# A fused attention and SwiGLU block: a new written-out instruction order for all five engines

## The chip, the cores and the metric

The kernel runs on one core of one Trainium2 chip. Its five engines work from queues of their own: TensorE (PE in the profile) multiplies matrices into PSUM, VectorE (DVE), ScalarE (ACT) and GpSimd (POOL) work on SBUF and PSUM, and SyncE (SP) issues DMA transfers. Each queue runs in order; semaphores hold an instruction until what it needs from another engine or a transfer is done. The metric is the device time of one execution in microseconds (us), lower is better.

## What is computed

```python
def reference(A_x, A_wqkv, A_wo, B_x, B_w1, B_w3, B_w2, c, w_mod):
    # x: 1 x 2048 x 512 in bf16; 32 heads of 16; window 8, dilation 2; F = 1792
    ...
    qkv = x @ wqkv                      # of the modulated layer norm of x
    idx = pos[:, None] - arange(8) * 2  # 8 keys behind each position, every second one
    logits = einsum('bhsd,bhswd->bhsw', q, k[idx]) * scale   # masked where idx < 0
    o = einsum('bhsw,bhswd->bhsd', softmax(logits), v[idx])
    attention = o @ wo
    ...
    out = (silu(h @ w1) * (h @ w3)) @ w2
```

The block around these two is an adaptive layer norm: a vector c gives, through w_mod, a shift, a scale and a gate for each half. So x becomes x + gate_a * attention(LN(x) * (1 + scale_a) + shift_a), and then x + gate_b * ffn(LN(x) * (1 + scale_b) + shift_b). The output is bf16 in the form of x.

## The kernel before, in words

The 2048 positions are 16 tiles of 128. Python code first records 1118 operations (class Program), each with its engine, and with the values that it reads and writes; nothing is issued yet. The recorded work goes through these stages.

First layer norm: statistics (L555, L556 on DVE), variance and power (L563, L565 on POOL), normalizing (L576 on DVE); then a transpose on PE (L636) or by DMA, and the modulation while draining (L644, L621 on ACT). Projections: q and k by L691 (drained by L700 and L701 on ACT), v by L711 (drained by L721), which goes to a scratch in HBM.

Attention, tile by tile and mostly two tiles to a softmax: the elementwise product of q with eight shifted k on DVE (L742, 128x4096), its sum over each head by tiled matmuls (L752; L749 for the first tile), maximum and subtraction on DVE (L764, L769), exp on ACT (L782), sum, reciprocal and scaling on DVE (L794, L796, L797), a transpose on PE (L807) with its copy on ACT (L811), the product with the gathered v on DVE (L827, 128x4096; the gathers are DMAs by L124 on SP), the sum over the window by tiled matmuls (L855), a copy on ACT (L861), a transposing DMA that SP issues (sb_ot), the output projection on PE (L867), and the residual with its row sum on DVE (L871).

Second layer norm, for two tiles at a time: POOL makes the negative mean (L586); ACT squares each of the two tiles with a row sum (L590); POOL makes the variance (L596), its power (L597) and the bias (L599); ACT normalizes each (L601). Then transposes (L636, or by DMA) and modulation (L644, L621). The FFN goes over six groups of tiles, two or four tiles each ([0,1], [2,3], [4..7], [8..11], [12,13], [14,15]): for each of 14 slices of F gate and up (L883, 128x256 or 128x512), silu on ACT (L889), the product on DVE (L892); then w2 (L921, L909 for the last two tiles), the addition on DVE (L931) and the store.

What sets the order of the work: a list, ORDER, written out at the end of the file, holds the numbers of the 1118 operations. `place` (L145) goes through it once and appends each operation to the queue of its engine, so ORDER sets each queue's sequence. A second list, SLOTS, says for each pooled value which buffer or PSUM bank it takes, and the values that share one follow each other in ORDER. `synchronize` then derives the waits: an operation waits for what it reads, and for the last users of a buffer that it takes over. Between engines nothing else is enforced; how two operations on different engines stand in ORDER has no meaning in itself.

```python
        for at, o in enumerate(self.placed):
            o.at = at
            o.pos = len(self.order[o.eng])
            self.order[o.eng].append(o)
            for v in o.vals:
                if v.pool is not None and v.pool.last.get(v.slot) is not v:
                    before = v.pool.last.get(v.slot)
                    if before is not None:
                        o.prev.extend(before.users)
                    v.pool.last[v.slot] = v
```

Of the kernel before, what the change touches and what calls it, by code (L numbers as in the profile page):

```python
# [272 lines left out]
def _build(p, A_x, A_wqkv, A_wo, B_w1, B_w3, B_w2, c, w_mod, out):  # L273
# [710 lines left out]
    143, 142, 144, 145, 90, 146, 147, 148, 107, 173, 171, 174, 108, 172, 109, 110, 111, 181, 179, 114, 115, 175, 176, 116, 125, 126,  # L984
    127, 128, 129, 130, 182, 121, 153, 180, 154, 156, 155, 112, 177, 150, 178, 149, 152, 151, 117, 135, 131, 132, 133, 134, 229,
    122, 123, 136, 137, 113, 183, 184, 185, 138, 186, 163, 164, 237, 161, 235, 165, 238, 139, 236, 187, 193, 140, 166, 227, 228,
    189, 239, 194, 195, 188, 41, 196, 197, 198, 190, 167, 331, 230, 332, 159, 287, 168, 240, 241, 242, 231, 232, 233, 246, 333, 289,
    157, 191, 192, 211, 118, 209, 288, 234, 244, 290, 199, 162, 339, 281, 158, 160, 347, 245, 212, 210, 243, 203, 205, 200, 215,
    216, 204, 349, 169, 348, 350, 279, 340, 218, 334, 280, 351, 206, 219, 282, 352, 353, 381, 341, 372, 291, 292, 293, 342, 207,
    294, 221, 354, 355, 250, 249, 362, 247, 369, 224, 213, 336, 248, 359, 361, 214, 201, 360, 257, 258, 283, 284, 285, 202, 371,  # L990
    356, 370, 357, 358, 253, 254, 208, 273, 276, 286, 259, 260, 170, 265, 266, 217, 261, 379, 298, 380, 363, 364, 222, 277, 365,
    220, 382, 373, 374, 43, 37, 375, 295, 255, 274, 263, 297, 296, 267, 223, 256, 264, 301, 411, 413, 270, 268, 335, 412, 49, 262,
    300, 366, 414, 299, 251, 252, 383, 415, 384, 275, 376, 302, 367, 368, 416, 385, 403, 271, 44, 417, 377, 378, 602, 603, 402, 404,
    604, 311, 312, 269, 303, 317, 318, 386, 387, 309, 310, 388, 304, 401, 418, 605, 307, 308, 606, 389, 390, 607, 609, 608, 337,
    278, 315, 392, 313, 314, 322, 325, 445, 225, 338, 615, 610, 614, 616, 394, 611, 393, 613, 612, 305, 391, 328, 306, 329, 443,
    316, 444, 405, 406, 319, 617, 622, 626, 407, 446, 627, 395, 396, 397, 419, 420, 623, 477, 45, 634, 635, 447, 642, 618, 272, 320,
    46, 636, 637, 628, 629, 619, 620, 621, 52, 226, 326, 51, 630, 631, 408, 624, 625, 344, 638, 448, 421, 422, 50, 640, 639, 641,
    662, 670, 644, 643, 645, 449, 409, 646, 410, 450, 632, 647, 47, 633, 654, 398, 399, 451, 663, 666, 400, 671, 672, 452, 48, 343,
    650, 655, 668, 667, 669, 648, 649, 682, 683, 684, 453, 652, 651, 653, 435, 656, 657, 664, 433, 436, 685, 454, 665, 673, 658,
    678, 434, 437, 321, 426, 686, 687, 689, 695, 688, 694, 691, 660, 323, 659, 661, 423, 478, 475, 696, 424, 438, 425, 697, 690,  # L1000
    692, 674, 693, 742, 439, 730, 465, 731, 466, 468, 743, 427, 744, 745, 726, 706, 708, 707, 709, 476, 479, 467, 469, 428, 458,
    429, 710, 711, 456, 457, 712, 713, 722, 723, 724, 727, 728, 729, 455, 732, 733, 440, 725, 430, 746, 698, 699, 459, 53, 702, 703,
    480, 54, 470, 471, 472, 734, 735, 441, 442, 460, 461, 345, 346, 714, 431, 432, 738, 762, 462, 481, 497, 482, 473, 474, 483, 675,
    676, 747, 763, 463, 464, 704, 498, 484, 764, 765, 499, 715, 487, 716, 717, 700, 701, 718, 720, 509, 770, 771, 679, 705, 750,
    736, 737, 490, 748, 772, 485, 719, 500, 749, 488, 721, 739, 740, 752, 741, 507, 766, 767, 769, 489, 779, 768, 751, 754, 753,
    486, 501, 773, 774, 778, 775, 776, 780, 777, 781, 782, 491, 785, 758, 759, 760, 327, 783, 755, 529, 502, 510, 508, 492, 784,
    798, 818, 511, 512, 503, 531, 532, 680, 830, 493, 513, 330, 530, 831, 521, 539, 832, 514, 515, 820, 822, 814, 799, 815, 522,
    819, 504, 505, 516, 517, 541, 494, 324, 520, 495, 518, 506, 834, 806, 786, 807, 496, 761, 836, 794, 833, 823, 835, 677, 821,
    838, 858, 808, 859, 681, 533, 534, 559, 519, 523, 535, 809, 837, 540, 558, 542, 543, 524, 860, 525, 570, 790, 796, 795, 788,
    797, 545, 861, 791, 810, 787, 789, 802, 792, 793, 526, 544, 536, 547, 546, 549, 548, 862, 537, 569, 538, 550, 803, 527, 528,  # L1010
    839, 863, 864, 804, 805, 811, 551, 594, 812, 813, 866, 824, 825, 867, 800, 567, 593, 552, 553, 554, 874, 592, 868, 869, 826,
    557, 816, 560, 801, 840, 827, 870, 871, 555, 872, 568, 556, 817, 876, 841, 865, 854, 875, 561, 873, 846, 877, 828, 571, 842,
    595, 881, 562, 572, 829, 577, 563, 584, 855, 879, 578, 579, 564, 573, 850, 856, 580, 574, 878, 880, 906, 908, 581, 596, 565,
    566, 575, 576, 954, 857, 585, 907, 583, 909, 918, 919, 894, 582, 586, 843, 956, 955, 957, 886, 887, 958, 756, 898, 587, 588,
    895, 597, 890, 891, 589, 926, 847, 598, 599, 959, 960, 962, 899, 900, 901, 927, 961, 848, 590, 600, 591, 601, 1032, 910, 920,
    921, 963, 964, 965, 892, 893, 967, 966, 1034, 928, 1033, 1035, 1036, 1037, 851, 968, 852, 849, 972, 974, 976, 978, 973, 980,
    929, 911, 984, 986, 977, 979, 975, 844, 845, 985, 987, 853, 1039, 988, 990, 989, 1038, 930, 931, 932, 981, 982, 983, 933, 902,
    904, 991, 903, 905, 970, 934, 969, 1040, 896, 897, 971, 882, 1041, 888, 889, 884, 883, 922, 885, 923, 935, 936, 924, 946, 1043,
    1042, 942, 937, 938, 950, 1004, 1006, 1005, 1007, 1000, 1045, 1002, 1001, 925, 1008, 1012, 1009, 1013, 1016, 1017, 996, 998,
    997, 914, 999, 915, 1018, 992, 1003, 1044, 993, 994, 1014, 1015, 1019, 995, 916, 757, 912, 917, 1024, 913, 939, 1028, 940, 1070,  # L1020
    1090, 1071, 1086, 1072, 1073, 1091, 1010, 1087, 1074, 1011, 1082, 1075, 1088, 941, 1083, 1078, 1089, 1079, 1092, 1093, 1094,
    1084, 1096, 1095, 1097, 1080, 1081, 943, 951, 1085, 952, 944, 947, 948, 949, 1054, 1050, 1066, 1051, 1052, 1053, 953, 945, 1020,
    1062, 1064, 1076, 1077, 1063, 1046, 1067, 1068, 1069, 1047, 1055, 1056, 1057, 1021, 1022, 1023, 1058, 1060, 1059, 1061, 1029,
    1048, 1025, 1098, 1049, 1030, 1065, 1099, 1100, 1101, 1110, 1111, 1112, 1114, 1115, 1113, 1116, 1117, 1026, 1027, 1102, 1031,
    1103, 1104, 1105, 1106, 1107, 1108, 1109,
]
SLOTS = [
    7, 0, 1, 2, 3, 4, 5, 6, 0, 1, 2, 3, 4, 5, 6, 7, 0, 1, 2, 3, 4, 5, 6, 7, 0, 3, 4, 5, 6, 0, 1, 1, 0, 2, 3, 0, 4, 0, 7, 1, 0, 2, 1,
    2, 3, 6, 1, 5, 0, 7, 5, 7, 6, 2, 2, 1, 4, 0, 1, 3, 1, 2, 0, 4, 1, 4, 0, 7, 5, 1, 3, 6, 3, 0, 4, 2, 0, 1, 2, 1, 1, 0, 2, 4, 0, 1,
    2, 1, 4, 3, 6, 5, 1, 1, 0, 1, 3, 2, 3, 2, 4, 0, 0, 2, 3, 4, 1, 0, 3, 5, 6, 5, 1, 5, 3, 3, 2, 2, 0, 2, 6, 1, 2, 0, 3, 6, 7, 5, 3,  # L1030
    0, 1, 1, 0, 6, 0, 1, 1, 0, 0, 0, 0, 0, 1, 1, 5, 1, 6, 0, 1, 1, 1, 0, 5, 1, 0, 3, 1, 5, 0, 2, 3, 1, 4, 0, 2, 4, 2, 100, 5, 1, 2,
    5, 1, 1, 0, 1, 4, 0, 7, 1, 0, 4, 0, 1, 1, 1, 1, 5, 0, 7, 0, 0, 1, 1, 6, 0, 1, 1, 1, 0, 5, 1, 0, 0, 100, 7, 0, 2, 1, 1, 6, 0, 2,
    6, 2, 100, 5, 1, 1, 3, 1, 3, 0, 2, 5, 0, 4, 1, 0, 0, 1, 0, 1, 6, 0, 0, 6, 1, 0, 4, 1, 7, 0, 2, 6, 6, 1, 0, 0, 1, 1, 6, 100, 2,
    0, 0, 2, 1, 4, 7, 2, 1, 5, 103, 2, 102, 3, 101, 6, 103, 1, 100, 4, 101, 5, 104, 2, 106, 4, 102, 3, 100, 3, 105, 2, 104, 1, 102,
    4, 105, 1, 100, 3, 108, 5, 104, 2, 109, 4, 105, 7, 110, 5, 102, 7, 113, 5, 103, 6, 111, 2, 102, 6, 107, 6, 101, 1, 112, 0, 100,
    3, 102, 0, 3, 2, 0, 4, 4, 104, 0, 101, 1, 105, 1, 102, 1, 105, 7, 115, 1, 103, 4, 116, 7, 100, 2, 100, 5, 101, 7, 105, 7, 101,
    5, 119, 2, 102, 1, 117, 7, 100, 7, 118, 5, 103, 2, 103, 4, 100, 5, 106, 5, 104, 4, 114, 2, 102, 0, 104, 6, 104, 4, 107, 2, 101,
# [38 lines left out]
```

## Time and profile before

| | us |
|---|---|
| median of 3 runs | 239.26 (239.23 to 241.12) |
| the profiled execution, its own time | 240.36 |
| span of the profiled execution, first to last instruction | 238.6 |
| the two transposing DMAs that the chain of waits goes through | 4.29 and 3.71 |

The granted TensorE clock is 1.00 throughout. In the profile's timeline a line gives the start in us, the duration, the engine, the line of the kernel, the operation, the tiles written and read, and how many alike stand in a row; in brackets stands how long the engine was idle before, and on whom it waited. The chain of waits is followed back from the last instruction: each line has a start, a share of time, and the engine and line that held the end at that moment.

### The profile page before, as it was taken

How to read it: one execution, taken by the hardware profiler on the slowest of the kernel's cores; microseconds unless marked ns; L12 is line 12 of the kernel's file. 1: busy time of each engine (PE TensorE's matmuls, PEld its weight loads, DVE VectorE, ACT ScalarE, POOL GpSimd, SP SyncE). 2: the span in 40 equal slices, each digit the busy share in tenths (PEclk: the TensorE clock that was granted, in tenths of full speed). 3: DMA queues.
4: the chain of work that ended last, by engine and by line, in shares of the span. 5: the costliest groups of instructions: out<-in, count | busy, mean ns of one | idle time of the engine just before them, and what ended most of it. 6: DMA issues, size and time to landing. Idle time of an engine off the chain costs nothing.

```text
span 238.6 us, 4560 instructions
## 1 busy us (share of the span) xinstructions
PE 232.2 (97%) x1806; PEld 136.7 (57%) x1806; DVE 179.4 (75%) x279; ACT 138.3 (58%) x267; POOL 28.8 (12%) x66
## 2 busy tenths in 40 slices
PE   7999999999999998999999999999899999999995
PEld 4776554545688683664444444444375457485874
DVE  5699999999999999899999999690653403434433
ACT  2289587899978737776765594747553406040300
POOL 4434000013002000240003420020010000000000
PEclk9999999999999999999999999999999999999999
DMA  6999999999999996876972783634303000000202
GB/s 216 372 330 309 157 242 301 217 288 315 302 293 254 247 203 178 240 180 193 229 220 62 192 209 76 166 113 46 67 5 104 3 0 0 3 22 0 69 1 88
DMA packets 46317, 38.85 MB, mean 163 GB/s; under 512 B 21704, under 2 KB 37080, under 8 KB 46296
## 3 DMA queue, kind: packets, MB, share of 16 engines
q1 hardware_dynamic: 46288, 38.56, 65.1%
q8 instruction: 14, 0.23, 0.4%
q14 instruction: 7, 0.06, 0.1%
q10 hardware_dynamic: 8, 0.00, 0.0%
HBM read 29.62 MB, written 4.21 MB: 142 GB/s over the span
## 4 chain that ended last, share of the span: by engine, by line
PE 83%; DMA 8%; DVE 3%; SPq 3%; ACT 1%; issue 0%
PE pall L883 40%; PE pall L921 17%; PE pall L691 7%; PE pall L867 5%; DMA sb_x<-in_A_x_dram 5%; PE pall L711 4%; DMA sb_ot<-sb_ac 3%; PE pall L752 3%; SPq L124 3%; PE pall L855 3%; PE pall L909 3%; DVE sb_pq L742 2%; DVE sb_st L555 1%; PE pall L807 1%; DVE sb_xn L576 1%; ACT sb_ac L861 0%
## 5 line engine op out<-in xcount | busy, mean ns | idle before, releaser
L883 PE MATMUL pall<-sb_h,sb_w 128*128 128x256 bf16 (+1 forms) x672 | 102.6, 308 | 0.0
L883 PEld LDWEIGHTS pall<-sb_h,sb_w 128*128 128x128 bf16 x672 | 65.0, 98 | 35.7 <-issue 2.5
L889 ACT ACTIVATE sb_sg<-pall 128x256 bf16<-128x256 f32 (+1 forms) x84 | 35.6, 454 | 54.5 <-PE pall L883 53.4
L892 DVE TENSOR_TENSOR sb_hh<-sb_sg,pall 128x256 bf16<-128x256 bf16 (+1 forms) x84 | 40.0, 505 | 36.1 <-PE pall L883 34.0
L921 PE MATMUL pall<-sb_w,sb_hh 128*128 128x512 bf16 x196 | 44.9, 379 | 0.0
L742 DVE TENSOR_TENSOR sb_pq<-sb_q,sb_kT 128x4096 bf16<-128x4096 bf16 x16 | 36.3, 2282 | 0.0
L921 PEld LDWEIGHTS pall<-sb_w,sb_hh 128*128 128x128 bf16 x196 | 19.0, 98 | 21.6 <-DVE sb_hh L892 0.4
L691 PE MATMUL pall<-sb_h,sb_wqkv 128*128 128x512 bf16 (+1 forms) x160 | 31.0, 336 | 0.0
L827 DVE TENSOR_TENSOR sb_vsh<-sb_vsh,sb_al 128x4096 bf16<-128x4096 bf16 x12 | 27.2, 2284 | 0.5 <-DMA sb_vsh<-v_scratch_dram 0.5
L621 ACT ACTIVATE sb_h<-sb_h,sb_modc 128x512 bf16<-128x512 bf16 (+1 forms) x24 | 16.5, 743 | 9.1 <-DMA sb_h<-sb_xn 9.1
L691 PEld LDWEIGHTS pall<-sb_h,sb_wqkv 128*128 128x128 bf16 x160 | 14.7, 98 | 11.7 <-ACT sb_ac L861 0.4
L931 DVE TENSOR_TENSOR sb_o<-pall,sb_x 128x512 bf16<-128x512 f32 (+1 forms) x18 | 11.1, 628 | 10.9 <-PE pall L921 7.1
L867 PE MATMUL pall<-sb_wo,sb_ot 128*128 128x512 bf16 x64 | 16.0, 379 | 1.9 <-DMA sb_ot<-sb_ac 1.9
L711 PE MATMUL pall<-sb_wqkv,sb_h 128*128 128x512 bf16 x64 | 16.0, 379 | 0.0
L644 ACT ACTIVATE sb_h<-pall,sb_modc 128x256 bf16<-128x256 bf16 (+1 forms) x18 | 9.9, 611 | 7.9 <-DVE sb_modc L509 6.9
L586 POOL TENSOR_SCALAR sb_nm<-sb_sx 128x2 f32<-128x2 f32 x8 | 1.7, 218 | 105.3 <-DVE sb_x L871 105.3
L861 ACT ACTIVATE sb_ac<-pall 128x512 bf16<-128x512 f32 x16 | 9.5, 595 | 7.1 <-PE pall L855 6.9
L601 ACT ACTIVATE sb_xn<-sb_x,sb_nb,sb_rs 128x512 bf16<-128x512 bf16 x16 | 12.4, 807 | 0.7 <-POOL sb_nb L599 0.6
L871 DVE SCALAR_TENSOR_TENSOR sb_x<-pall,sb_x 128x512 bf16<-128x512 f32 x16 | 10.8, 686 | 2.2 <-PE pall L867 2.1
L590 ACT ACTIVATE sb_xn<-sb_x,sb_nm 128x512 bf16<-128x512 bf16 x16 | 11.4, 714 | 1.8 <-POOL sb_nm L586 1.8
L721 ACT ACTIVATE sb_v<-pall 128x512 bf16<-128x512 f32 x16 | 9.6, 605 | 2.8 <-PE pall L711 2.8
L555 DVE BATCH_NORM_STATS2 sb_st<-sb_x 128x6 f32<-128x512 bf16 x16 | 10.5, 679 | 0.7 <-DMA sb_x<-in_A_x_dram 0.6
(87 smaller groups left out, 209.5 us busy)
## 6 DMA issues: line engine op xcount, KB each, us to landing
sb_vsh<-v_scratch_dram SPq DMA_DIRECT2D x48, 256.0 KB, 5.2
sb_vshx<-v_scratch_dram SPq DMA_DIRECT2D x16, 256.0 KB, 4.4
sb_w<-in_B_w_dram SPq DMA_DIRECT2D x6, 512.0 KB, 7.6
sb_w<-in_B_w_dram SPq DMA_DIRECT2D x6, 384.0 KB, 4.2
v_scratch_dram<-sb_v SPq DMA_DIRECT2D x16, 128.0 KB, 6.1
out_dram<-sb_o SPq DMA_DIRECT2D x14, 128.0 KB, 1.8
sb_wqkv<-in_A_wqkv_dram SPq DMA_DIRECT2D x6, 256.0 KB, 6.3
sb_x<-in_A_x_dram SPq DMA_DIRECT2D x4, 256.0 KB, 6.5
```

The lines of the kernel that those rows point to most:

```text
L555: o = p.op("dve", lambda e, T=T: e.bn_stats(st[:, T, :], x_sb[:, T, :]), 595, ("st", T), r=[vx[T]], w=[vs])
L601: p.op("act", lambda e, vn=vn, T=T: e.activation(vn.at[:], x_sb[:, T, :], ACT.Identity, bias=nb[:, T, :], scale=rs[:, NT + T, :]), c_act(5 ...
L621: return e.activation(vh.at[:, ft, 0:n * P], vh.at[:, ft, 0:n * P], ACT.Identity, bias=modc[:, 8 * which + ft:8 * which + ft + 1], scale=m ...
L691: ins = e.matmul(bank(vp)[:, j * n:(j + 1) * n], wqkv[:, t, col:col + P], vh.at[:, t, 0:n], start=(t == ORDER[0] and j == 0), stop=(t == O ...
L711: ins = e.matmul(bank(vp), vh.at[:, t, tt * P:(tt + 1) * P], wqkv[:, t, 2 * D:3 * D], start=(t == ORDER[0]), stop=(t == ORDER[-1]))
L742: return e.tensor_tensor(vp.at[:], in0, in1, ALU.mult)
L827: return e.tensor_tensor(v_w, v_w, a_w, ALU.mult)
L867: ins = e.matmul(bank(vy), vt.at[:, ft, :], wo[:, ft, :], start=(ft == 0), stop=(ft == KT - 1))
L883: ins = e.matmul(bank(vp)[:, 0:n], wt[:, t, fi * P:(fi + 1) * P], vh.at[:, t, 0:n], start=(t == 0), stop=(t == KT - 1))
L889: p.op("act", lambda e: e.activation(vt.at[:, 0:n], bank(vgp)[:, 0:n], ACT.Silu), c_act(n), k, r=[vgp], w=[vt], table="silu")
L892: p.op("dve", lambda e: e.tensor_tensor(vh_.at[:, 0:n], vt.at[:, 0:n], bank(vup)[:, 0:n], ALU.mult), c_dve(n), k, r=[vt, vup], w=[vh_])
L921: ins = e.matmul(bank(vz), vhh[fi].at[:, tt * P:(tt + 1) * P], w2[:, fi, :], start=(fi == 0), stop=(fi == NF - 1))
```

## The change

Only ORDER, from its fourth row on, and SLOTS are new: the numbers of operations stand in another sequence, and pooled values take other buffers and banks. No operation, tile, load or rule for waits is new. The new lists come from a search over sequences, with twenty random draws of hold-ups in the queues. The rows of the list that hold the second layer norm of tiles 0 and 1 (602 is L586, 603 and 604 are L590, 605 to 607 are L596, L597 and L599, 608 and 609 are L601):

```diff
-    300, 366, 414, 299, 251, 252, 383, 415, 384, 275, 376, 302, 367, 368, 416, 385, 403, 271, 44, 417, 377, 378, 602, 603, 402, 404,
-    604, 311, 312, 269, 303, 317, 318, 386, 387, 309, 310, 388, 304, 401, 418, 605, 307, 308, 606, 389, 390, 607, 609, 608, 337,
-    278, 315, 392, 313, 314, 322, 325, 445, 225, 338, 615, 610, 614, 616, 394, 611, 393, 613, 612, 305, 391, 328, 306, 329, 443,
-    316, 444, 405, 406, 319, 617, 622, 626, 407, 446, 627, 395, 396, 397, 419, 420, 623, 477, 45, 634, 635, 447, 642, 618, 272, 320,
...
+    413, 273, 411, 414, 412, 252, 270, 394, 335, 367, 300, 302, 415, 403, 299, 383, 384, 385, 274, 368, 377, 378, 602, 271, 603,
+    256, 315, 316, 604, 303, 304, 392, 605, 606, 607, 269, 307, 308, 305, 313, 404, 386, 314, 322, 416, 608, 609, 387, 388, 389,
+    319, 610, 390, 401, 614, 445, 417, 320, 306, 309, 611, 613, 612, 615, 617, 402, 616, 391, 311, 272, 393, 328, 329, 325, 443,
...
```

What this makes of three queues around that place (a line of the kernel for each operation, in the queue's order):

```
ACT before   L782 L590 L590 L701 L701 L700 L700 L700 L811 L601 L601 L701 L721 L644
ACT after    L590 L700 L701 L590 L700 L700 L701 L601 L601 L811 L782 L721 L700 L644
DVE before   L871 L769 L871 L794 L796 L797 L794 L493 L742 L494 L742 L827 L827
DVE after    L871 L871 L794 L769 L796 L797 L742 L742 L827 L794 L796 L797 L827
POOL, both   L586 L596 L597 L599
```

Elsewhere: near the start PE's queue has one L711 and then two L636 behind 24 L691, where it had two L711, two L691 and then L636. The four L636 that follow the second layer norm of tiles 0 and 1 stood together before, in pairs of matmuls; now an L691 stands between the two tiles' transposes. The matmuls of L883 (FFN), L855, L867 and L921 are interleaved in another sequence throughout; the copy L861 of tile 6 stands behind an exp (L782) on ACT, and one L586 behind the L597 and L599 of the pair before it on POOL. SP's issues of weight loads, gathers and transposing DMAs leave in another sequence. The 14 runs of tiled matmuls and the 10 table loads of ACT stay as many.

## The prediction

> **What bounds the kernel now.** First the page's busy times, slices and chain:
>
> ```profile
> PE 232.2 (97%) x1806; PEld 136.7 (57%) x1806; DVE 179.4 (75%) x279; ACT 138.3 (58%) x267; POOL 28.8 (12%) x66
> PE   7999999999999998999999999999899999999995
> DVE  5699999999999999899999999690653403434433
> PE 83%; DMA 8%; DVE 3%; SPq 3%; ACT 1%; issue 0%
> ```
>
> PE is the bound: 97% of the span, 83% of the chain. DVE is as full in the first two thirds, so there a late DVE result can stop PE; in the last third nothing but PE counts. An order can therefore only win what PE stands still, and can lose without limit. So I took PE's timeline next, start to start: a 128x512 matmul steps by 0.216 us and a 128x256 by 0.109, entering a run of tiled matmuls (L752, L855) costs 0.09 more, and what is left over is a stall. After the first 9 us there are three:
>
> ```profile
> 90.82 1.03 PE L867 MATMUL pall<-sb_wo,sb_ot 128*128 128x512 bf16 x4
> 92.04 0.61 PE L855 MATMUL pall<-sb_vsh,sb_ind 128*32 128x512 bf16 x8 [0.19 <-DVE sb_vsh L827]
> ...
> 93.90 0.60 PE L883 MATMUL pall<-sb_h,sb_w 128*128 128x256 bf16 x4
> 95.54 1.02 PE L867 MATMUL pall<-sb_wo,sb_ot 128*128 128x512 bf16 x4 [1.04 <-DMA sb_ot<-sb_ac]
> ...
> 166.51 1.03 PE L867 MATMUL pall<-sb_wo,sb_ot 128*128 128x512 bf16 x4
> 168.35 1.04 PE L867 MATMUL pall<-sb_wo,sb_ot 128*128 128x512 bf16 x4 [0.81 <-DMA sb_ot<-sb_ac]
> ```
>
> They are 92.04 − 90.82 − 0.86 − 0.09 = 0.27; 95.54 − 93.90 − 0.44 = 1.20; 168.35 − 166.51 − 0.86 = 0.98: together 2.45 us. The chain of waits says what the larger two wait for: the output projection L867 needs the transposing DMA that its own tile's L855 set off a few us before.
>
> ```profile
> 91.12 4.29 DMA sb_ot<-sb_ac
> ...
> 164.59 3.71 DMA sb_ot<-sb_ac
> ```
>
> **The change part by part.** Operations, tiles, loads and their counts are the same (14 runs of tiled matmuls and 10 table loads in both), so only stalls differ. I laid the new queue of each engine end to end with the steps above and asked of each operation when its inputs are there.
>
> *Gains.* Before, L867 of tiles 7, 14 and 15 came 5.72, 5.09 and 6.49 us after their L855, for 7 and 15 with the stall in it, so this is what the way takes at most (copy 0.6, transposing DMA 3.7 to 4.3, issue); after, 6.4, 5.3 and 12.25 us of PE work stand between. L855 of tile 6 comes at least 0.2 behind its product. All three stalls go: −2.45.
>
> *The head.* The transposes L636 of tiles 2 and 3 move up, behind one L711 after 24 L691. PE gets there at about 11.69, and the normalized tile is there at 11.89 (L576 of DVE): +0.22, between 0 (the write seen earlier) and 0.45 (a second tile as late).
>
> *Second layer norm of tiles 0 and 1.* This is the main term. Its chain runs ACT square, square (L590), POOL L596, L597, L599, ACT normalize (L601), PE transposes (L636). Before:
>
> ```profile
> 51.52 0.72 ACT L590 ACTIVATE sb_xn<-sb_x,sb_nm 128x512 bf16<-128x512 bf16 x1 [0.33 <-POOL sb_nm L586]
> ...
> 52.24 0.71 ACT L590 ACTIVATE sb_xn<-sb_x,sb_nm 128x512 bf16<-128x512 bf16 x1
> ...
> 52.94 1.06 ACT L701 ACTIVATE sb_kT<-pall 128x512 bf16<-128x512 f32 x2
> ```
> ```profile
> 53.12 0.19 POOL L596 TENSOR_SCALAR sb_rs<-sb_var 128x2 f32<-128x2 f32 x1 [1.63 <-ACT sb_xn L590]
> 53.39 0.70 POOL L597 TENSOR_TENSOR sb_rs<-sb_rs,sb_cst 128x2 f32<-128x2 f32 x1
> 54.17 1.83 POOL L599 TENSOR_TENSOR sb_nb<-sb_nm,sb_rs 128x2 f32<-128x2 f32 x1
> ...
> 129.06 2.10 POOL L596 TENSOR_SCALAR sb_rs<-sb_var 128x2 f32<-128x2 f32 x1 [6.64 <-ACT sb_xn L590]
> ```
> ```profile
> 50.48 0.68 DVE L871 SCALAR_TENSOR_TENSOR sb_x<-pall,sb_x 128x512 bf16<-128x512 f32 x1
> ...
> 53.67 2.28 DVE L742 TENSOR_TENSOR sb_pq<-sb_q,sb_kT 128x4096 bf16<-128x4096 bf16 x1
> ...
> 55.94 2.28 DVE L742 TENSOR_TENSOR sb_pq<-sb_q,sb_kT 128x4096 bf16<-128x4096 bf16 x1
> ```
>
> A small POOL operation takes 0.19 to 0.22 us (L597 0.70), but one that is issued while DVE is in a 128x4096 product (L742, L827) lasts until that product is over: L599 at 54.17 took 1.83 and ended at 56.00, the product at 55.95; L596 at 129.06 took 2.10 and ended at 131.16, a product that began at 128.82 at 131.10. The products always take 2.28 to 2.29, so POOL alone pays. The Trainium skill (SBUF — State Buffer, section "SBUF: two separate sides") has this as a rule: DVE and GpSimd share a pair of ports under an exclusive lock, whoever starts first keeps it for the whole instruction, and the other fully blocks. By it the term below is 3.0 to 3.3; were POOL merely slowed here and there it would be 0; the rows agree with the rule.
>
> Count from t, the start of the second residual L871 (50.48 before, about 50.35 after). Before, L596 came at t + 2.64 and the product of tile 7 at t + 3.19, so L596 and L597 got in first and only L599 was held. After, ACT does two drains (L700, L701, 0.48 each by the row at 52.94) between the two squares: first square t + 1.04, +0.72, +0.96, and 0.88 from the second square to L596: t + 3.60. In DVE's queue one L794 and two L493/L494 leave the stretch ahead of the product: 0.61 + 0.60 + 0.61 + 0.59 + 0.61 (L871, L794, L769, L796, L797) = t + 3.02. So L596 comes 0.58 after the product has begun and is held to t + 5.30. L597 then falls behind the product of tile 6, which follows at once, until t + 7.5, and L599 after it. If POOL gets its turn between two products, as it did at 56.00, the first L601 starts at t + 8.28; if the next product shuts it out again, at t + 8.65, and not later, since that product (L827 of tile 3) waits for L811, which stands behind L601 in ACT's queue. With 0.76 for L601 the tile is there at 59.4 to 59.75. PE's transposes come due at 55.99 by the laid queue + 0.44 (the head's 0.22 and a later step) = 56.43: a stall of 3.0 to 3.3, I take 3.2. It can't be a gain, since PE had no stall there; what lets it be 0 is the rival of the POOL chain that slips in. A late exp or residual shifts both sides of this race together, so the 0.58 doesn't depend on t.
>
> *Behind that stall.* Queued behind L601 on ACT are L811, an exp, drains and L644; the first silu comes after a table load (1.28 us by the row at 93.32), and the bank that L855 of tile 2 needs waits for it: +0.25 (0 to 0.5). The transposes of the second FFN group have no slack left in PE's queue: +0.1; the first matmul of the third FFN group follows its four L621 closely: +0.25. The two: +0.35 (0 to 0.7).
>
> *Nothing for the rest.* The L861 copy of tile 6 now stands behind an exp and its table load on ACT, so its transposing DMA leaves later; 0 to 1.1, and I take 0 since PE has other FFN matmuls queued ahead of its L867. SP's queue: weight loads and value gathers (L124) leave in another sequence; all land ahead of their use except the last gather of tile 5 (about 78.0 against 77.3), which the 3.2 us stall hides and which costs 0.2 if the stall isn't there. POOL: one L586 moves behind L597/L599 of the pair before, off the path. After 80 us every DVE result that PE needs is there 1 us or more ahead. The tail ends alike: four runs of 14 L909, an add, a store.
>
> Sum: 240.36 − 2.45 + 0.22 + 3.2 + 0.25 + 0.35 = 241.93 against the profiled 240.36 (span 238.6 and 1.8 around it), that is +1.57. The profiled execution stands 1.1 above the median 239.26; the difference goes to the median: 240.8. If those 1.1 us are stalls of that execution alone, the gain is smaller than 2.45 by so much and the time 241.9; both ends of the terms give 239.8 to 242.3.
>
> **The rivals.**
> *Held twice.* The layer norm of tiles 6 and 7 has the same race: L596 is held by a product until about 102.97, L597 runs 103.1 to 103.8, L599 comes at 103.87, and the next product starts at 103.83. If L599 loses, it is held to 106.05, and the normalize, L811 behind it, an L827 and the next FFN group come late: +2.2 (2.1 to 2.4), 243.0. For it: 0.04 us the wrong way; against it: that is less than my laying out can tell, and before, the same L599 was free (0.20 at 104.05).
> *The POOL chain slips in ahead of the first product* (the other side, faster). L596 has to come 0.58 earlier against the product, by drains that find their place later in the queue or a product that waits. Then the stall is gone: 240.36 − 2.45 + 0.22 + 0.25 + 0.35 + 0.2 = 238.93, that is −1.43: 237.8. It decides at L596 = start of the product. For it: 0.58 us is one DVE step; against: both move with the same residual.
> *PE's clock falls in the stall, or a further stall opens* (tile 6's transpose, up to 1.1). The granted clock is 1.00 in every stretch, also where PE stood still 1.2 us at 94; 3.2 us is longer than any stretch in this trace. By the 1.1 it is 241.9, by a second stall of 3.2 us 244.0; I take 243.0. The Trainium skill (TensorE: Matmul & The Clock Gate, section "What's actually happening") has the clock halved after an idle window of about 3.4 us and back after as much busy time; as an estimate from that page it would cost 1.7 us more, and a 3.2 us stall is just short of it; no run here shows it.
>
> **How the numbers follow.** Held once 0.47 (240.8); held twice 0.27 (243.0); slips in 0.16 (237.8); clock or further stall 0.10 (243.0). The likeliest is held once, 240.8, its own range 239.8 to 242.3. The range 237.8 to 243.5 takes in both neighbours and leaves out half of the slip-in (0.08), the upper edge of held twice (0.05) and a part of the last case (0.04): about 0.2. About 1% is what a measurement here can tell from no change: 236.87 to 241.65. Faster by more: the better third of slips in, 0.05. Slower by more: held twice 0.27, the last 0.10, and a good quarter of held once (0.13): 0.50. Within: 0.45.
>
> **What would show it.** Right: L596 of tiles 0 and 1 lasting 1.5 us or more beside the first of two products, L601 at about 58.6 to 59, and a gap of some 3 us ahead of L636 on PE with ACT named; no L867 <- DMA sb_ot among PE's waits near 94 and 167. Wrong: L596 of 0.19 ahead of the product (slips in), L599 of about 2 us near 104 (held twice), a granted clock under 1.00, or a stall at a place not named here.

## The result, and the profile after

| | us | granted clock |
|---|---|---|
| kernel before, median of 6 | 239.25 (238.44 to 241.12) | 1.00 in the profiled execution |
| changed kernel, median of 6 | 247.99 (246.16 to 249.47) | 1.00 once, 0.992 to 0.993 twice, 0.986 three times |
| profiled execution of the changed kernel | 247.27, span 245.6 | 0.993 |

The ratio is 1.036, 95% interval 1.030 to 1.042: slower by 8.7 us, outside the range 237.8 to 243.5.

The page after, the lines that answer to those shown of before:

```profile
PE 231.5 (94%) x1779; PEld 136.4 (56%) x1806; DVE 179.1 (73%) x279; ACT 139.1 (57%) x267; POOL 33.0 (13%) x66
PE   7999999795999999998699999999999999999995
DVE  5699999975979999996989999975444542225342
PEclk9999999999799999999999999999999999999999
PE 47%; ACT 3%; DMA 1%; POOL 1%; issue 1%; SPq 0%; DVE 0%
```

PE's work is the same (27 matmul records are missing, so its busy time is a little low), but there are holes in slices 8 and 10 and near slice 20, the clock dips in slice 11, and POOL is busy 4.2 us longer with the same 66 instructions. (The chain of after could be followed back only to 113 us, so its shares add up to about half of the span.) The waits of PE name the places:

```profile
PE pall L636 <- ACT sb_xn L601: 3.0, 1, 3.0
PE pall L867 <- DVE pall L769: 1.3, 1, 1.3
...
PE pall L883 <- ACT sb_h L621: 1.2, 1, 1.2
PE pall L855 <- DVE sb_vsh L827: 1.1, 1, 1.1
PE pall L855 <- DVE sb_vshx L827: 0.7, 1, 0.7
```

L867 no longer waits for tiles 7, 14 and 15. Start to start, with the steps of the prediction, PE's lost time in the profiled executions comes to this (the sum is that of the spans, 245.6 − 238.6):

| place | after, against before, us | forecast |
|---|---|---|
| head and projections, to 40 us of PE's work | −0.5 | +0.22 |
| ahead of L867 of tile 0 (49.14) | +1.5 | 0, not named |
| ahead of L636, second layer norm of tiles 0 and 1 (60.29) | +3.16 | +3.2 |
| low clock behind it | +1.7 | a rival, 0.10 |
| ahead of L867 of tile 7 and L855 of tile 6 | −1.3 | −1.47 |
| ahead of L855 of tiles 9 and 8 and the first L883 of the third FFN group (117 to 121) | +3.2 | +0.25; a rival, +2.2 |
| ahead of L867 of tile 15, and small steps | −0.8 | −0.98 |
| sum | +7.0 | +1.57 (with 0.35 of small terms) |

PE's timeline at the two largest holes of the first 65 us (one of the four L711 at 46.79 has no record, so PE was due at 46.79 + 0.86 = 47.65 and at 56.27 + 0.86 = 57.13):

```profile
46.79 1.04 PE L711 MATMUL pall<-sb_wqkv,sb_h 128*128 128x512 bf16 x3
49.14 1.89 PE L867 MATMUL pall<-sb_wo,sb_ot 128*128 128x512 bf16 x8 [1.31 <-DVE pall L769]
...
56.27 1.03 PE L711 MATMUL pall<-sb_wqkv,sb_h 128*128 128x512 bf16 x4
60.29 0.48 PE L636 MATMUL pall<-sb_ident,sb_xn 128*128 128x128 bf16 x4 [3.00 <-ACT sb_xn L601]
60.56 1.91 PE L691 MATMUL pall<-sb_h,sb_wqkv 128*128 128x512 bf16 x4
```

The 3.16 came about as forecast. The queues of POOL, ACT and VectorE in the changed kernel:

```profile
54.68 1.72 POOL L596 TENSOR_SCALAR sb_rs<-sb_var 128x2 f32<-128x2 f32 x1 [2.60 <-ACT sb_xn L590]
56.48 2.63 POOL L597 TENSOR_TENSOR sb_rs<-sb_rs,sb_cst 128x2 f32<-128x2 f32 x1
59.19 0.20 POOL L599 TENSOR_TENSOR sb_nb<-sb_nm,sb_rs 128x2 f32<-128x2 f32 x1
```
```profile
52.11 0.72 ACT L590 ACTIVATE sb_xn<-sb_x,sb_nm 128x512 bf16<-128x512 bf16 x1 [0.50 <-POOL sb_nm L586]
...
52.83 0.58 ACT L700 ACTIVATE sb_q<-pall 128x512 bf16<-128x512 f32 x1
53.31 0.59 ACT L701 ACTIVATE sb_kT<-pall 128x512 bf16<-128x512 f32 x1
53.79 0.72 ACT L590 ACTIVATE sb_xn<-sb_x,sb_nm 128x512 bf16<-128x512 bf16 x1
...
59.42 1.52 ACT L601 ACTIVATE sb_xn<-sb_x,sb_nb,sb_rs 128x512 bf16<-128x512 bf16 x2 [3.37 <-POOL sb_nb L599]
```
```profile
51.07 0.69 DVE L871 SCALAR_TENSOR_TENSOR sb_x<-pall,sb_x 128x512 bf16<-128x512 f32 x1 [0.16 <-PE pall L867]
...
54.07 4.48 DVE L742 TENSOR_TENSOR sb_pq<-sb_q,sb_kT 128x4096 bf16<-128x4096 bf16 x2
```

With t = 51.07, L596 comes at t + 3.61 (forecast 3.60) and the product starts at t + 3.00 (3.02). L596 of 0.19 us lasts 1.72, to the end of the first product (54.07 + 2.24 = 56.3). L597 comes 0.2 us after the second product began, and it lasts 2.63 instead of 0.70. L601 starts at t + 8.35 (8.28 to 8.65). Behind the hole PE runs at half rate (in each row, the number behind the five busy times is the granted clock):

```profile
60.00:61.00 1.00, 0.71 (x6) 0.43 (x7) 0.00 (x0) 1.00 (x3) 0.00 (x0) 0.74 1.10 345
61.00:62.00 1.00, 1.00 (x4) 0.43 (x3) 0.55 (x1) 1.00 (x3) 0.00 (x0) 0.50 1.10 347
62.00:63.00 1.00, 0.90 (x6) 0.57 (x5) 1.00 (x1) 1.00 (x3) 0.00 (x0) 0.50 1.10 348
63.00:64.00 1.00, 0.88 (x3) 0.36 (x3) 1.00 (x2) 1.00 (x3) 0.00 (x0) 0.56 1.09 347
64.00:65.00 1.00, 1.00 (x6) 0.42 (x5) 0.93 (x3) 0.72 (x2) 0.00 (x0) 1.00 1.02 306
```

That is 0.52 + 2 + 0.88 = 3.4 us at 0.50. The Trainium skill (TensorE: Matmul & The Clock Gate, section "What's actually happening") has a window of about 3.4 us for this; the length agrees. Its condition, an idle window of that length, does not quite: PE stood still 3.0 us.

The second hole is the rival "held twice". In POOL's queue L599 of tiles 6 and 7 lost its race by 0.12 us to the product that started at 110.03:

```profile
108.26 1.03 POOL L596 TENSOR_SCALAR sb_rs<-sb_var 128x2 f32<-128x2 f32 x1 [1.85 <-ACT sb_xn L590]
109.37 0.70 POOL L597 TENSOR_TENSOR sb_rs<-sb_rs,sb_cst 128x2 f32<-128x2 f32 x1
110.15 2.23 POOL L599 TENSOR_TENSOR sb_nb<-sb_nm,sb_rs 128x2 f32<-128x2 f32 x1
```

The layer norm after that one was held twice too (L596 of 2.02 us at 132.88, L597 of 2.63 at 134.99), and none of PE's waits belongs to it: being held costs time only where the result is due.

### The profile page after: what moved, and what is told of

The parts are those of the page before. It is cut to its first block, busy times and chain, and to the rows that moved or that the text cites. A ratio compares the mean times of both kernels' runs of the same rounds, so it can differ in the third digit from the quotient of the medians.

```text
span 245.6 us, 4527 instructions
## 1 busy us (share of the span) xinstructions
PE 231.5 (94%) x1779; PEld 136.4 (56%) x1806; DVE 179.1 (73%) x279; ACT 139.1 (57%) x267; POOL 33.0 (13%) x66
## 4 chain that ended last, share of the span: by engine, by line
PE 47%; ACT 3%; DMA 1%; POOL 1%; issue 1%; SPq 0%; DVE 0%
PE pall L883 27%; PE pall L921 12%; PE pall L867 3%; PE pall L909 2%; DMA sb_h<-sb_xn 1%; ACT sb_h L621 1%; PE pall L855 1%; PE pall L752 1%; POOL sb_rs L596 1%; ACT sb_xn L601 1%; ACT sb_xn L590 1%; ACT sb_sg L889 0%; POOL sb_rs L597 0%; SPq L124 0%; PE pall L807 0%
## 5 line engine op out<-in xcount | busy, mean ns | idle before, releaser
L883 PE MATMUL pall<-sb_h,sb_w 128*128 128x256 bf16 (+1 forms) x666 | 102.1, 308 | 1.6 <-ACT sb_h L621 1.2
L883 PEld LDWEIGHTS pall<-sb_h,sb_w 128*128 128x128 bf16 x672 | 64.8, 98 | 37.1 <-issue 2.1
L892 DVE TENSOR_TENSOR sb_hh<-sb_sg,pall 128x256 bf16<-128x256 bf16 (+1 forms) x84 | 39.8, 504 | 33.9 <-PE pall L883 23.9
L921 PE MATMUL pall<-sb_w,sb_hh 128*128 128x512 bf16 x186 | 43.6, 379 | 0.5
L691 PE MATMUL pall<-sb_h,sb_wqkv 128*128 128x512 bf16 (+1 forms) x156 | 31.4, 344 | 0.8 <-DMA sb_wqkv<-in_A_wqkv_dram 0.3
L827 DVE TENSOR_TENSOR sb_vsh<-sb_vsh,sb_al 128x4096 bf16<-128x4096 bf16 x12 | 27.4, 2286 | 5.1 <-ACT sb_al L811 3.2
L921 PEld LDWEIGHTS pall<-sb_w,sb_hh 128*128 128x128 bf16 x196 | 18.9, 98 | 21.5 <-ACT sb_sg L889 0.4
L621 ACT ACTIVATE sb_h<-sb_h,sb_modc 128x512 bf16<-128x512 bf16 (+1 forms) x24 | 16.5, 734 | 10.2 <-DMA sb_h<-sb_xn 10.2
L691 PEld LDWEIGHTS pall<-sb_h,sb_wqkv 128*128 128x128 bf16 x160 | 15.0, 100 | 12.5 <-issue 1.1
L601 ACT ACTIVATE sb_xn<-sb_x,sb_nb,sb_rs 128x512 bf16<-128x512 bf16 x16 | 12.4, 806 | 12.9 <-POOL sb_nb L599 12.9
L586 POOL TENSOR_SCALAR sb_nm<-sb_sx 128x2 f32<-128x2 f32 x8 | 1.8, 219 | 123.6 <-DVE sb_x L871 123.6
L867 PE MATMUL pall<-sb_wo,sb_ot 128*128 128x512 bf16 x61 | 15.3, 379 | 1.5 <-DVE pall L769 1.3
L711 PE MATMUL pall<-sb_wqkv,sb_h 128*128 128x512 bf16 x60 | 15.2, 379 | 0.3 <-ACT sb_q L700 0.2
L590 ACT ACTIVATE sb_xn<-sb_x,sb_nm 128x512 bf16<-128x512 bf16 x16 | 11.4, 713 | 6.4 <-POOL sb_nm L586 6.3
L861 ACT ACTIVATE sb_ac<-pall 128x512 bf16<-128x512 f32 x16 | 9.1, 596 | 5.4 <-PE pall L855 5.3
L701 ACT ACTIVATE sb_kT<-pall 128x512 bf16<-128x512 f32 x16 | 9.4, 600 | 3.4 <-PE pall L691 3.3
```

The lines of the kernel that those rows point to most:

```text
L590: p.op("act", lambda e, vn=vn, T=T: e.activation(vn.at[:], x_sb[:, T, :], ACT.Square, bias=nm[:, T, :], accum_out=var[:, T, :]), c_act(512 ...
L601: p.op("act", lambda e, vn=vn, T=T: e.activation(vn.at[:], x_sb[:, T, :], ACT.Identity, bias=nb[:, T, :], scale=rs[:, NT + T, :]), c_act(5 ...
L621: return e.activation(vh.at[:, ft, 0:n * P], vh.at[:, ft, 0:n * P], ACT.Identity, bias=modc[:, 8 * which + ft:8 * which + ft + 1], scale=m ...
L691: ins = e.matmul(bank(vp)[:, j * n:(j + 1) * n], wqkv[:, t, col:col + P], vh.at[:, t, 0:n], start=(t == ORDER[0] and j == 0), stop=(t == O ...
L711: ins = e.matmul(bank(vp), vh.at[:, t, tt * P:(tt + 1) * P], wqkv[:, t, 2 * D:3 * D], start=(t == ORDER[0]), stop=(t == ORDER[-1]))
L827: return e.tensor_tensor(v_w, v_w, a_w, ALU.mult)
```

## The experiments

Each ran on one chip beside the kernel before, whose median was 240.0 in runs 1 to 4, 239.5 in 5 to 7, 240.0 in 8 and 9, 240.3 in run 10 and 239.9 in the last two. The changed kernel was not timed again beside them; a time set against its 247.99 is good to about 1 us, which is what the medians of the kernel before differ by (239.25 to 240.26). Theory: POOL is shut out by the products in two places, the clock falls behind holes, and L867 of tile 0 waits for its transposing DMA. The rivals stand in each expectation.

**1. The two squares next to each other** (numbers in ORDER; 604 is the second L590):

```diff
-    603, 256, 315, 316, 604, 303,
+    603, 604, 256, 315, 316, 303,
```

> The changed kernel with one number of the order moved: the second square (L590, tile 1) directly behind the first, so the two drains no longer stand between them on ScalarE. Theory (POOL shut out by the product): L596 comes at t + 2.64 after the start t of the second residual, ahead of the product at t + 3.0, L597 starts at t + 2.91 and runs beside it, only L599 is held, L601 starts near t + 5.5, and the 3.0 us stall ahead of L636 falls to 0.1; with it goes the low clock behind it. Time 243.1 (the execution of the changed kernel at clock 1.00, 246.16, less 3.0). If L597 loses its race by the 0.09 us, the stall is 2.1 and the time 245. Rival (the late drains or the late residual themselves hold the layer norm, the product is no matter): at most the 0.96 us of the two drains goes, 247.0.

Measured: 244.44, ratio 1.019 (1.014 to 1.024); 243.4 and 243.8 in the two executions at clock 1.00. POOL's three operations:

```profile
53.81 0.19 POOL L596 TENSOR_SCALAR sb_rs<-sb_var 128x2 f32<-128x2 f32 x1 [1.63 <-ACT sb_xn L590]
54.09 0.70 POOL L597 TENSOR_TENSOR sb_rs<-sb_rs,sb_cst 128x2 f32<-128x2 f32 x1
54.87 1.64 POOL L599 TENSOR_TENSOR sb_nb<-sb_nm,sb_rs 128x2 f32<-128x2 f32 x1
```

L597 got in 0.08 us ahead of the product (54.17), and the hole ahead of L636 is gone. Two drains of 0.96 us in the wrong place cost 3.5 us: far more than their own time, so the rival falls. In the profiled execution the clock now fell later, at 117 to 120, behind the three smaller holes.

**2. The drains alone, in the kernel before:**

```diff
-    404, 604, 311, 312, 269, 303, 317, 318, 386,
+    404, 311, 312, 269, 303, 317, 318, 604, 386,
```

> The kernel before with one number moved: the second square of the same pair goes behind the two L701 drains that followed it, the rest as before. Theory (shut out): L596 comes at about 54.1, 0.4 after the product of 53.67 began, is held to 56.0, L597 then falls behind the next product and L599 perhaps behind the one after; L601 starts at 59.0 to 60.4 instead of 56.04, so PE stalls 1.9 to 3.4 us ahead of L636, and the clock may fall for 3.4 us behind it: 241.2 to 244.4. Rival (only the drains' own time counts): at most 0.96 us, 239.3 to 240.2.

Measured: 245.58, ratio 1.025 (1.021 to 1.030), clock 0.986 to 0.993 in all. One number moved makes 5.6 us, more than expected. L596, L597 and L599 lasted 1.91, 2.70 and 1.61 us, L636 waited twice (3.3 and 0.4 us), and the clock was low for 6.8 us instead of 3.4.

**3. The transposing DMA ahead of two weight loads** (47 and 43 are the loads, 366 and 376 the DMAs of tiles 0 and 1):

```diff
-    295, 47, 225, 226, 363, 364, 365, 43, 380, 366, ... 301, 376, 278,
+    295, 225, 226, 363, 364, 365, 380, 366, ... 301, 376, 47, 43, 278,
```

> The changed kernel with the two weight loads (512 and 384 KB) that SP issues just ahead of the transposing DMA of tile 0 moved behind the one of tile 1. Theory (the 1.26 us stall ahead of the first L867 is that DMA, issued at 44.01 and landed at 49.01): it is issued near 42.4 and lands before PE is due at 47.9, the stall goes, and everything behind comes 1.1 to 1.26 earlier: 246.8. Rival (the stall is VectorE's L769 or the scaled wo, as the profile's wait names VectorE): the stall stays and the time is that of the changed kernel, 248.0.

Measured: 246.84, ratio 1.028 (1.023 to 1.033), as expected; L867 of tile 0 does not wait at all. Its DMA left 1.3 us after the tile's L855, where it had left 3.6 us after it, and the two DMAs landed within 2.7 to 3.1 us instead of 3.7 to 5.0. So the wait that the profile of the changed kernel put down to VectorE's L769, the last of several semaphores, was a DMA: issued at 44.01, landed at 49.01, L867 at 49.14. The profiles of runs 4, 5 and 6, where SP's queue is as in the changed kernel, name that DMA themselves. There and in run 1 the hole is 0.45 to 0.77 us instead of 1.5, since PE comes later: L867 starts at 48.8 to 49.2 in all five, against 48.2 to 48.9 in the kernel before and in runs 2 and 12, which have its head. So this place and the head have to be read together, and cost about 0.6 us in the mean.

This run's trace shows one thing more. The hole ahead of L636 is as long as in the changed kernel, but the clock behind it stayed at 1.00; the low stretch of this execution (0.993) lies at 8.5 to 11.9 us, behind a wait of 1.26 us in the head.

```profile
60.83 0.40 PE L636 MATMUL pall<-sb_ident,sb_xn 128*128 128x128 bf16 x4 [2.99 <-ACT sb_xn L601]
61.06 1.03 PE L691 MATMUL pall<-sb_h,sb_wqkv 128*128 128x512 bf16 x4
```

**4. Matmuls in the hole:** an added operation ahead of L636.

```diff
+        for i in range(12):
+            ins = e.matmul(bank(vfill), ident[:], wo[:, 0, :], start=True, stop=True)
```

> The changed kernel with twelve added 128x512 matmuls (2.6 us) just ahead of the first L636 of the second layer norm, into the bank that those transposes take; their result is read by nobody. They run while PE would stand still 3.0 us, so they cost nothing there. Theory (the clock falls because PE stands still about 3 us): the granted clock stays 1.00 in every execution, and the time is that of the changed kernel's execution at clock 1.00: 246.2, against a median of 248.0. Rival (the clock falls for another cause, such as the load or the time since the start): 0.986 to 0.993 as in the changed kernel and 248.0.

Measured: 245.20, ratio 1.023 (1.019 to 1.026), clock 1.00 in three of four executions (244.9 to 245.3); the fourth was at 0.986. PE works 2.6 us more, and the kernel is 2.8 us faster. About 1 us of that is not the clock's: at clock 1.00 the changed kernel took 246.16 in its one such execution. PE's timeline (one of the twelve added matmuls has no record):

```profile
56.76 2.75 PE L975 MATMUL pall<-sb_wo,sb_ident 128*128 128x512 bf16 x11
59.92 0.40 PE L636 MATMUL pall<-sb_ident,sb_xn 128*128 128x128 bf16 x4 [0.40 <-ACT sb_xn L601]
60.15 1.03 PE L691 MATMUL pall<-sb_h,sb_wqkv 128*128 128x512 bf16 x4
```

The four L691 behind L636 take 1.03 us to the end of the last, and took 1.91 in the changed kernel (60.56). So the hole can bring the clock down, but does not always: behind a hole of about 3 us the clock was halved in three of four traces (the changed kernel, runs 2 and 6; not run 3), and with the hole filled it was not, in the one trace there is.

**5. More work for VectorE ahead of the first product:**

```diff
+    for i in range(3):
+        p.op("dve", lambda e, i=i: e.bn_stats(st[:, i, :], x_sb[:, NT - 1, :]), 595, ("hold", i), w=[Val("st")])
```

> The changed kernel with three needless BN_STATS (L972 here, 0.61 us each, one operand in SBUF, their result read by nobody) put on VectorE just ahead of the first of the two products; the drains stay between the squares. Theory (shut out): the product starts at t + 4.8 instead of t + 3.0, so L596 (t + 3.6), L597 and L599 (t + 4.65) all run at their 0.2, 0.7 and 0.2 us ahead of it, L601 starts near t + 5.05 instead of t + 8.35, and the 3.0 us stall ahead of L636 goes, with the low clock behind it. The products are 1.8 us later, so L855 of tile 3 comes due about 1.1 us before its input. Net 1.9 and some clock: 244.5 to 246 although VectorE has 1.8 us more to do. Rival (what delays the layer norm is the late drains and residual): L601 stays at t + 8.3 or comes later, the time is 248.0 to 249.8.

Measured: 245.01, ratio 1.021 (1.015 to 1.028). With the drains where the change put them, POOL is free at once and the hole ahead of L636 is gone:

```profile
54.50 0.19 POOL L596 TENSOR_SCALAR sb_rs<-sb_var 128x2 f32<-128x2 f32 x1 [2.60 <-ACT sb_xn L590]
54.78 0.70 POOL L597 TENSOR_TENSOR sb_rs<-sb_rs,sb_cst 128x2 f32<-128x2 f32 x1
55.56 0.19 POOL L599 TENSOR_TENSOR sb_nb<-sb_nm,sb_rs 128x2 f32<-128x2 f32 x1
```

1.8 us of useless work on a busy engine made the kernel 3 us faster. Together with 1 and 2 this settles it: the race with the product is the cause, not the lateness.

**6. The second race** (717 is an L892, 507 and 509 the products of tiles 10 and 11):

```diff
-    487, 717, 778, ... 507, 753, 737, 755,
+    487, 778, ... 507, 753, 737, 717, 758, 754, 755,
```

(758 and 754 are matmuls of L921 that need the moved L892; PE's queue stays as it was.)

> The changed kernel with one L892 (0.33 us) moved on VectorE from ahead of the products of tiles 10 and 11 to between them. Theory (L599 of tiles 6 and 7 lost its race with the second of these products by 0.12 us): the first product ends 0.33 earlier and frees L596 so much earlier, the second starts when it did, so L599 comes 0.2 ahead of it and takes 0.2 instead of 2.23; the three stalls of 0.86, 1.30 and 1.26 us near 117 to 121 shrink to about 1 together, and no low clock falls there. Time 245.0 to 245.7 against 248.0. Rival (those stalls come from the DMA transposes or from VectorE being full): L599 may be short and the time stays within 0.5 of 248.0.

Measured: 246.26, ratio 1.026 (1.019 to 1.034), at clock 0.986 to 0.993 in all executions. L599 took 0.19 us at 111.05, and the three holes are gone, but L921 now waits 1.0 us for the moved L892. Less than the expected gain: the moved L892 stood last of three there (run 10 has it first), and in the trace the clock was low for 6.8 us behind the first hole, not 3.4.

**7. Mends 1, 3 and 6 together.**

> The changed kernel with three mends together: the two squares next to each other, the transposing DMAs ahead of the two weight loads, and the L892 between the two products. Theory (the three stalls and the low clock behind them are the whole loss, and the gains that the laid queues promised are there): 248.0 - 3.2 - 1.26 - 3.4 - about 2 of clock = 238.1, between 237.4 and 239.0, so 0.5 to 2.5 below the kernel before. Rival (further waits of the new order are hidden under these stalls and show when they go): 240 to 242.

Measured: 244.05, ratio 1.015 (1.010 to 1.021). Neither expectation held, since mend 3 undid mend 1. ACT's timeline shows it:

```profile
52.35 0.60 ACT L721 ACTIVATE sb_v<-pall 128x512 bf16<-128x512 f32 x1 [1.89 <-PE pall L691]
52.84 0.71 ACT L590 ACTIVATE sb_xn<-sb_x,sb_nm 128x512 bf16<-128x512 bf16 x1
```

The loads, moved one place too little, now stood ahead of a store of v (landed at 52.26 instead of about 50.1), whose buffer this L721 needs; both squares stood behind it, L596 came at 54.43 against a product at 52.71, and a hole of 2.1 us opened.

**8 and 9. The loads one place further back; then two ways around the races.** Run 8 keeps the squares together and has one product wait; run 9 leaves the drains between and has both products wait.

```diff
+    prods[7].deps[p.ops[607]] = True
+    prods[11].deps[p.ops[775]] = True
```

(Both lines in run 9, the second alone in run 8; 607 and 775 are the two L599.)

> The changed kernel with the two squares next to each other, the two weight loads one place further back in SP's queue than in the run before (behind the store of v of tile 11, whose late landing held an L721 and so both squares there), and the second of the products of tiles 10 and 11 made to wait for L599 of tiles 6 and 7 (a wait of 0.3 us on VectorE, which stood idle 2.1 us right behind that product) instead of the moved L892. Theory (three places are the whole loss): against the run with the three first mends at clock 1.00 (242.9) the 1.01 us ahead of L711, 2.0 of the 2.08 ahead of L636 and the 1.19 ahead of L921 go: 238.7, within 1 us of the kernel before (239.5), and the clock stays 1.00. Rival (a fourth wait shows when these go): 240 to 242.

> The changed kernel with the drains left between the squares, the loads back as in the run beside it, and both first-hit products made to wait for the L599 of their layer norm: the product of tile 7 for that of tiles 0 and 1, the product of tile 11 for that of tiles 6 and 7. Theory (shut out): all of L596, L597 and L599 take 0.2, 0.7 and 0.2 us, VectorE loses 1.8 us at the first place, L855 of tile 3 is late by about 1.1 and L807 by 0.4 as with the three BN_STATS; no stall of 3 us, no low clock: 1.5 above the run beside it, 240.2. Rival (lateness of the drains): a stall of 2 to 3 us ahead of L636 stays and the time is 242 or more.

Measured: 243.04, ratio 1.013 (1.009 to 1.016), and 243.12, ratio 1.014 (1.009 to 1.019). No L601 holds PE any more in either, so the races are out of the way; but both lie 3 us above the kernel before, run 8 above both of its expectations, and run 9 where its rival had it, without the rival's stall. New waits stand in their place: in run 8, L827 of tile 3 waits 2.0 us for its last gather, with holes of 1.1 and 0.4 us on PE behind it, and the first L883 of the third FFN group waits 2.2 us for L621.

```profile
59.36 2.29 DVE L827 TENSOR_TENSOR sb_vsh<-sb_vsh,sb_al 128x4096 bf16<-128x4096 bf16 x1 [2.01 <-DMA sb_vsh<-v_scratch_dram]
```

**10. The order of the transfers:** the squares together, the moved L892 first of three, and in SP's queue the gathers for tile 3 ahead of those for tile 2, loads behind both.

```diff
-    47, 43 | 394, 403, 392, 404, 401, 402, 391, 393 | 45, 44, 46
+    403, 404, 401, 402, 394, 392, 391, 393 | 43, 45, 44, 46, 47
```

(Only the loads and gathers of SP's queue are written here, in its order; between them a store of v, 269, keeps its place in the middle. The other two edits are as in runs 1 and 6.)

> The changed kernel with the squares next to each other, the L892 moved from ahead of the products of tiles 10 and 11 to between them (as the first of three), and SP's queue mended: the gathers of v for tile 3 all ahead of those for tile 2, the two weight loads behind both, as the kernel before has them in the main. Theory (what the last runs lacked is the order of the transfers: L827 of tile 3 waited 2.0 us for its last gather, and that made the stalls of 1.0 and 0.4 us ahead of L855 and L807): that gather lands by 56, the product starts at 57.3, these stalls go, and so does the one of 2.1 ahead of L636; some 0.5 us stays ahead of L921 near 107. Time 239.2, within 1 us of the kernel before. Rival (the transfers as a whole are late, not this gather): the wait goes over to the weights of the first L883 or to the transposes of tiles 6 and 7, and the time stays at 241.5 to 243.

Measured: 243.52, ratio 1.012 (1.007 to 1.017); 242.1 to 244.1 at clock 1.00. L827 of tile 3 started at 57.60 without a wait and its two holes are gone, as the theory has it, but the time is the rival's, or a little more: now L827 of tile 5 waits 1.65 us for a gather (hole 1.6), and the third FFN group still 2.0.

**11. Two more of the kind**, on top of run 10: the gathers for tile 5 ahead of the others, and eight L883 from ahead of L867 of tiles 7 and 6 to behind them.

```diff
-    423, ... 433, ... 434, ... 435, 426,
+    433, ... 434, ... 435, 423, 426,
...
-    766, 736, 716, 483, 345, 473, 474, 767, 715, 463, 464,
+    766, 483, 345, 473, 474, 767, 715, 463, 736, 716, 464,
```

(736 and 716 are the L883, 473 and 463 the L867.)

> The run with the mended gathers of tile 3, and two mends more: the gathers of v for tile 5 all ahead of the two for tile 4 that stood among them, and eight L883 moved from ahead of L867 of tiles 7 and 6 to behind them, so that the second layer norm of these tiles comes up to 0.87 us earlier. Theory (each stall that showed has its own cause in a queue's order): L827 of tile 5 no longer waits 1.65 us for its last gather, and the 1.5 us ahead of its L855 go; L867 of tile 6 waits some 0.5 us for its transposing DMA, and the 2.0 us ahead of the first L883 of the third FFN group fall to about 1.2. Time 240.3 against 242.2 at clock 1.00 of the run before. Rival (PE, once freed, is held by the transfers wherever it is): the waits move on, 241.5 to 242.5.

Measured: 240.84 in 12 executions, all at clock 1.00, ratio 1.006 (1.003 to 1.008). That is 7 us below the changed kernel with nothing changed but the order of four queues, and still 0.9 above the kernel before. L827 of tile 5 waits 0.56 us, no longer 1.65. What is left on PE's timeline, at L867 of tiles 7 and 6:

```profile
96.26 1.47 PE L883 MATMUL pall<-sb_h,sb_w 128*128 128x256 bf16 x12
98.27 1.02 PE L867 MATMUL pall<-sb_wo,sb_ot 128*128 128x512 bf16 x4 [0.54 <-DMA sb_ot<-sb_ac]
99.90 1.02 PE L867 MATMUL pall<-sb_wo,sb_ot 128*128 128x512 bf16 x4 [0.60 <-DMA sb_ot<-sb_ac]
```

Holes of 0.70 and 0.76, and none ahead of the third FFN group. So the 1.2 us that the change had won at tile 7 was not to be had: with L867 late, the FFN group starved; with L867 earlier, the wait of before is back.

**12. One gain taken into the kernel before** (600 is L867 of tile 15):

```diff
-    590, 600, 591, 601, 1032, 910, 920, 921,
+    590, 591, 910, 920, 600, 601, 1032, 921,
```

> The kernel before with a single gain of the change taken over: L867 of tile 15 moved behind the next two groups of four L883 (1.73 us), as the change has it further back. Theory (late in the kernel PE alone is the bound, so a removed stall is a gain): the wait of 0.98 us for the transposing DMA at 167 goes and nothing takes its place: 0.9 to 1.0 below the kernel before. Rival (the stall shows again elsewhere, in the layer norm of tiles 14 and 15 or their FFN group): within 0.3 of the kernel before.

Measured: 239.30, ratio 0.997 (0.994 to 1.000), so 0.6 us below the kernel before by the medians and 0.8 by the ratio, with an interval that reaches just to no change. The wait is gone and nothing replaces it:

```profile
167.44 1.03 PE L867 MATMUL pall<-sb_wo,sb_ot 128*128 128x512 bf16 x4
168.30 1.89 PE L883 MATMUL pall<-sb_h,sb_w 128*128 128x512 bf16 x8
170.03 1.03 PE L867 MATMUL pall<-sb_wo,sb_ot 128*128 128x512 bf16 x4
```

It is the only kernel here that came out below the kernel before beside it. The profiled execution is not shorter (span 238.6 in both): its head ran 0.9 us later, which shows in L867 of tile 14, at 167.44 instead of 166.51.

## Why the prediction was wrong, point by point

- **The main term was right.** The shut-out POOL chain, its offsets from t to 0.02 us and its hole (3.2 forecast, 3.16 measured) stand; runs 1, 2 and 5 show the cause.
- **The step that failed: the sum has room for one new wait, and puts every other at nothing or deals it out as a rival.** Held once, held twice and a fallen clock had 0.47, 0.27 and 0.10 and one time each, as if only one could be. All three happened in one execution, and they are not independent, since the clock fell behind the hole; a fourth wait, at tile 0, stood at nothing. The forecast 241.93 for the profiled execution, with the measured 1.5 (tile 0), 1.7 (clock), 3.2 − 0.25 (held twice) and −0.7 (the head, −0.5 where +0.22 stood) put in, is 247.4, against 247.27 measured. The range was built from the same chances, so it ended far below.
- **"against it: that is less than my laying out can tell".** A dead heat of 0.04 us the wrong way was given 0.27 and a cost of 2.2; it lost by 0.12. At the main term the same laying out was good to 0.02 us, which speaks for a higher chance, but one place shows no more than that. The holes there cost 3.2; run 6, where L599 gets in, loses them and gains a wait of 1.0.
- **The clock.** The text took a stall of 3.2 us to be just short of what brings the clock down, and the clock fell behind 3.0 to 3.3 us idle in three of four traces. Of the changed kernel's six executions five have a mean clock under 1.00, but only one of them has a trace; where the clock fell in the others is not shown.
- **"Nothing for the rest": SP's queue.** Tile 0's transposing DMA, behind two weight loads where the kernel before has one, is not named there: 1.5 us in the profiled execution, 0.45 to 0.77 in four others. That every other transfer lands in time held only because of the hole. With the hole mended the late gathers of tiles 3 and 5 showed (runs 8 and 10), where the prediction had 0.2 for the one and nothing for the other.
- **The mis-sized term: +0.25 ahead of the third FFN group.** Even with its L599 free, that group waits 2.0 to 2.2 us (runs 8 and 10). It is the price of the late L867 of tiles 7 and 6, which the gains counted as −1.2: in run 11, with these L867 earlier, that wait is gone and theirs is back.
- **The gain late in the kernel was right:** where PE alone is the bound, the 0.98 of tile 15 is a gain, in run 12 too. The head's +0.22 does not show (−0.5); the executions differ there by more than that, so its size stays open.
- **A sum that does not come out:** the upper ends of the terms add up to 241.8 for the median, or 242.9 with the 1.1 us taken as stalls, and not to 242.3. It changes nothing above.

Left open: what decides whether the clock falls behind a hole, and for 3.4 or 6.8 us.

## What to carry to other kernels

When a queue is reordered, follow small operations of an engine that shares a resource with long ones of another: a race lost by a tenth of a microsecond (0.12 here) costs the rest of the long operation, and before a pair of long operations it can cost both. Waits in a full pipeline are not alternatives: sum those that the laid queues show, add what a hole brings with it, and ask of every mend which wait stands behind it. A stall that goes late in the kernel, where one engine alone is the bound, was a gain here (run 12); the one that went in the crowded part had been somebody else's slack (run 11).

## What the runs showed of the hardware that was not expected

- A POOL operation that is issued just after a product of VectorE began waits through it: L597, 0.70 us when free, was issued at 56.48, 0.2 us into the second product, and lasted 2.63 us. The one that waited already (L596, to 56.40) got its turn where the first product ended, though the second followed at once.
- The granted clock falls by whole stretches of 3.4 us at 0.50: one in the traces of the changed kernel (60.5 to 63.9) and of runs 1, 5 and 10 (117.1 to 120.5) and 3 (8.5 to 11.9), two on end in runs 2 and 6. A mean clock of 0.993 is one of them (3.4 × 0.5 / 245 = 0.007), 0.986 two.
- No length of one idle stretch of PE decides it. The clock fell behind 3.0 us (the changed kernel, run 6), 3.3 (run 2), 2.0 (run 10) and behind stretches of 0.71, 1.15 and 1.13 us with work between them (run 1), and in the head behind 1.26 (run 3). It did not behind 3.0 in run 3, 2.2 in run 8, and 0.71, 1.15 and 1.16 in the changed kernel. The kernel before shows a mean clock of 0.985 to 0.993 in 11 of its 63 executions beside the runs; its one trace, at 1.00, has no idle stretch of PE above 1.3 us.
